# Attention and MLP on one core: the second products of a block queued straight behind its first products, in place of being mixed with the next block's first products

## The chip, the cores and the metric

The kernel runs on one core of a Trainium2 chip. The metric is device time in microseconds of one execution, the median of several runs.

## The reference

An attention over 8 batches, 12 heads, 448 positions of 64 values feeds an MLP with a squared ReLU:

```
scores = (q @ k^T) / sqrt(64);  e = exp(scores - m)
attn   = e / (sum(e) + exp(-m) + 1e-9)          # softmax with one added to the sum
x      = (attn @ v), heads put side by side     # 3584 tokens x 768
g      = max(x @ w_in, 0) ** 2                  # 3584 x 2048
out    = g @ w_out                              # 3584 x 768, float32
```

## The kernel before

**Attention.** The work is cut into units `(b, pr, q0, n)`: batch, pair of heads, first query, number of queries. Batch 0 is done in 12 half units of 192 and 256 queries, batches 1 to 7 in 6 units of 448 queries each, so `NU` is 54 and the main loop runs over `i` from 0 to 54. In turn `i` TensorE does `scores(u, et, 0)` and `scores(u, et, 1)` of the unit `i` (tile `sp`, L174 in batches 0 and 1, L186 from batch 2 on), then for the unit before it the row sums (tile `mp`, L230) and the values (tile `xp`, L222). ScalarE takes the exponential of each score tile (`et`, L154), and makes the reciprocal of the row sums with a logarithm and an exponential (`lnz` L233, `rcp` L234). VectorE adds the chunks of `et` in three steps (`es`, L199 and L201), and `normalise` (L242) multiplies `xp` by `rcp` into `xt`, which is the input of the MLP.

**MLP.** It runs over blocks of tokens: 128, 256 (both of batch 0), then 512 and 384 in turn, the last of 512. `mlp_in` makes the first products: 16 tiles of 6 matmuls each (L257), each tile cleared at zero by VectorE (`rt`, L266) and squared by it (`g`, L268). Only in the first block ScalarE does `rt`. `mlp_out` makes the second products: for each 128 tokens 16 matmuls of 512 columns and 16 of 256 (L280), each tile scaled by ScalarE into `ot` (L284), and then stored by SyncE (L296). A block's first products need `xt` of its tokens; its second products need all 16 tiles of its `g`.

**Buffers.** The row sums (`zp`), the tiles of both products and the transposes of batches 0 and 1 all take their PSUM tiles in turn from one pool, `m_psum`, of three buffers. Scores have two buffers (`s_psum`), the values one (`x_psum`), `g` two for each of its names.

**Order.** The order is written out by hand (`manual_schedule`), and every engine executes its own instructions in program order. The MLP is a filler: `mlp_in` and `mlp_out` are generators that yield after every matmul with its nominal time (columns / 2.4 in ns), and `drain(ns)` lets the queued work run until that much has been issued. A turn spends its `share` in five parts:

```
scores(u, et, 0); drain(share * 0.45); scores(u, et, 1)
row_sums(prev, pes); values(prev, pet, xp, 0); values(prev, pet, xp, 1)
drain(share * 0.15)
for step in range(3): add_chunks(...); drain(share * (0.15, 0.1, 0.15)[step])
normalise(prev, xp, rcp)
```

`ready` says after which unit which work is queued; `share` is then the work left, divided by six. In the kernel before, `ready` queues the first products of a block together with the second products of the block before it, and `queue` puts both into one generator, `mixed`. It takes the one whose done share is smaller and lets it go on to the end of its PSUM tile (the flag that the generators yield beside the time). So the second products of a block come some six turns after its first products, and after the last turn there remain a mixed piece (second products of 384 tokens, first products of 512) and the second products of 512.

**Loads.** GpSimd loads `v`, the weights and the copies `stage` of q and k; SyncE loads q and k transposed from `stage` (L129, `transposed_loads`, after the unit `pr` = 2 of the batch before), and stores the output on the same queue.

Of the kernel before, what the change touches and what calls it, by code (L numbers as in the profile page):

```python
# [15 lines left out]
def kernel(  # L16
# [12 lines left out]
    NT, DM = out.shape  # L29
    DF = moe_w_in.shape[1]  # L30
    NPAIR = H // 2
    DCH = DM // 128
    NFFB = DF // 128
# [41 lines left out]
    def load_v(b, p0, p1):  # L75
        hs = slice(2 * p0, 2 * p1)
        if b not in vns:
            vns[b] = v_pool.tile([P, H, RUN, D], FP16, name="vn")
        nc.gpsimd.dma_start(out=vns[b][:, hs], in_=v_r[b, :, hs])  # L79
# [29 lines left out]
    def stage(b):  # L109
        for n, t in (("q", q), ("k", k)):  # L110
            st = nc.dram_tensor(f"stage_{n}{b}", (TOTAL,), FP16, kind="Internal").ap()
            stages[n, b] = st
            src = t.rearrange("b h s d -> (b h s d)")
            lo = b * HSD - FRONT
            hi = min(lo + TOTAL, B * HSD)
            m = (hi - lo) // 1024 * 1024
            for x, y in ((lo, lo + m), (lo + m, hi)):
                if y > x:
                    w = min(y - x, 1024)
                    nc.gpsimd.dma_start(out=st[x - lo:y - lo].rearrange("(r w) -> r w", w=w),  # L120
                                        in_=src[x:y].rearrange("(r w) -> r w", w=w))
            if hi < lo + TOTAL:
                nc.gpsimd.dma_start(out=st[hi - lo:TOTAL].rearrange("(r w) -> r w", r=1),
                                    in_=src[0:lo + TOTAL - hi].rearrange("(r w) -> r w", r=1))
# [11 lines left out]
    def regroup(b, pr):  # L136
        for name in "qk":
            f = flat.tile([P, RUN, 2, D], FP16, name=f"flat{name}")
            nc.vector.tensor_copy(f, naturals[name, b, pr].rearrange("p h t d -> p t h d"))
            flats[name, b, pr] = f  # L140

    def transposes(b, pr):
        tp = m_psum.tile([128, 2, 512], FP16, name="mp")
        for i, name in enumerate("qk"):
            for s in range(RUN):
                nc.tensor.transpose(tp[:, i, P * s:P * s + P], flats[name, b, pr][:, s], ident[0:P, 0:P])
        if b not in qks:
            qks[b] = qk_pool.tile([128, 3, COLS], FP16, name="qk")
        nc.vector.tensor_copy(qks[b][:, 0:2, pr * S:(pr + 1) * S], tp[:, :, 0:S])
# [92 lines left out]
        nc.vector.tensor_mul(xts[b // 2][:, pr, c:c + n], xp[:, 0:n], rcp[:, 0:n])  # L242

    gts = {}

    def mlp_in(t0, n):
        gt = gts[t0] = []
        xt, x0 = xts[t0 // (2 * S)], t0 % (2 * S)  # L250
        per = max(1, 512 // n) if n < 384 else 1
        for f0 in range(0, NFFB, per):
            hp = m_psum.tile([128, 512], FP32, name="mp")
            for j in range(per):
                fb = f0 + j
                for dc in range(DCH):
                    nc.tensor.matmul(hp[:, j * n:(j + 1) * n], win[:, dc, fb * 128:(fb + 1) * 128],  # L257
                                     xt[:, dc, x0:x0 + n], start=(dc == 0), stop=(dc == DCH - 1))
                    if j < per - 1 or dc < DCH - 1:
                        yield n / 2.4, False  # L260
            m = per * n
            rt = r_pool.tile([128, 512], FP16, name="rt")
            if t0 == 0:
                nc.scalar.activation(out=rt[:, 0:m], in_=hp[:, 0:m], func=AF.Relu)  # L264
            else:
                nc.vector.tensor_scalar(out=rt[:, 0:m], in0=hp[:, 0:m], scalar1=0.0, scalar2=None, op0=ALU.max)  # L266
            g = g_pool.tile([128, 512], FP16, name=f"g{f0}")
            nc.vector.tensor_mul(g[:, 0:m], rt[:, 0:m], rt[:, 0:m])  # L268
            for j in range(per):
                gt.append(g[:, j * n:(j + 1) * n])  # L270
            yield n / 2.4, True

    def mlp_out(t0, n):
        gt = gts.pop(t0)
        for ts in range(n // 128):
            ot = osb_pool.tile([128, DM], FP32, name="ot")
            for n0, n1 in ((0, 512), (512, DM)):
                op = m_psum.tile([128, 512], FP32, name="mp")
                for fb in range(NFFB):
                    nc.tensor.matmul(op[:, 0:n1 - n0], gt[fb][:, ts * 128:(ts + 1) * 128], wout[:, fb, n0:n1],  # L280
                                     start=(fb == 0), stop=(fb == NFFB - 1))
                    if fb < NFFB - 1:
                        yield (n1 - n0) / 2.4, False
                nc.scalar.activation(out=ot[:, n0:n1], in_=op[:, 0:n1 - n0], func=AF.Copy, scale=OUT_SCALE)  # L284
                if n1 < DM:
                    yield (n1 - n0) / 2.4, True
            c = t0 + ts * 128
            end = c + 128
            while c < end:
                b = c // S  # L290
                step = RUN if b in ON_PE else 2
                rows = out[b * S:(b + 1) * S, :].rearrange("(p t) m -> t p m", t=step)
                t, p = c % S // (S // step), c % (S // step)
                m = min(S // step - p, end - c)
                o = c + 128 - end
                nc.sync.dma_start(out=rows[t, p:p + m, :], in_=ot[o:o + m, :])  # L296
                c += m
            yield (DM - 512) / 2.4, True


    warm = consts.tile([128, 512], FP16)
# [24 lines left out]

    work, left = [], [0.0]

    def mixed(parts):

        gens = [[0.0, total, gen] for gen, total in parts]
        while gens:
            g = min(gens, key=lambda g: g[0] / g[1])
            for ns, end in g[2]:
                g[0] += ns
                yield ns
                if end:
                    break
            else:
                gens.remove(g)  # L340

    def queue(parts):
        both = []
        for part, t0, n in parts:
            total = (NFFB * DCH * n if part == 1 else n // 128 * NFFB * DM) / 2.4
            both.append(((mlp_in if part == 1 else mlp_out)(t0, n), total))
            left[0] += total
        work.append(mixed(both))

    def drain(ns):  # L350
        while work and ns > 0:
# [9 lines left out]
    units += [(b, pr, 0, S) for b in range(1, B) for pr in range(NPAIR)]  # L361
    NU = len(units)

    ready = {NPAIR - 1: [(1, 0, 128)], 2 * NPAIR - 1: [(1, 128, 256), (2, 0, 128)]}
    last, t0 = (2, 128, 256), 384
    for b in range(1, B):
        n = 384 if b % 2 == 0 else 512
        ready[(b + 2) * NPAIR - 1] = [last, (1, t0, n)]
        last = (2, t0, n)
        t0 += n  # L370


    regroup_at = {pr - 2: (0, pr) for pr in range(2, NPAIR)}
    transpose_at = {pr - 1: (0, pr) for pr in range(1, NPAIR)}
# [4 lines left out]
    def keep_warm(n):  # L379
        wp = m_psum.tile([128, 512], FP32, name="mp")  # L380
        for _ in range(n):
            nc.tensor.matmul(wp, warm[:, 0:128], warm, start=True, stop=True)
# [8 lines left out]
    for i in range(NU + 1):  # L391
        u = units[i] if i < NU else None
        prev = units[i - 1] if i > 0 else None
        xp = rcp = None
        if prev:
            pet, pes = et, es
            xp = x_psum.tile([128, 512], FP32, name="xp")
        if u:
            b, pr = u[0:2]
            if pr == 0 and 0 < b and b + 1 < B:  # L400
                load_v(b + 1, 0, NPAIR)
                stage(b + 1)
            et = e_pool.tile([P, RUN * 2 * S], FP16, name="et")
            es = e_pool.tile([P, 4 * S], FP16, name="es")
            scores(u, et, 0)
            if i == 0:
                keep_warm(8)
            if i in transpose_at:
                transposes(*transpose_at[i])
            if i in regroup_at:  # L410
                regroup(*regroup_at[i])
            if i < NPAIR:
                keep_warm(1)
            drain(share * 0.45)
            scores(u, et, 1)
        if prev:
            rcp = row_sums(prev, pes)
            values(prev, pet, xp, 0)
            values(prev, pet, xp, 1)
            if i < NPAIR:  # L420
                keep_warm(1)
        drain(share * 0.15)
        for step in range(3):
            if u:
                add_chunks(u, et, es, step)
            drain(share * (0.15, 0.1, 0.15)[step])
        if prev:
            normalise(prev, xp, rcp)
            if i - 1 in ready:
                queue(ready[i - 1])  # L430
                share = left[0] / NPAIR
        if u and b and pr == 2 and b + 1 < B:
            transposed_loads(b + 1)
    queue([last])
    drain(1e12)


# [28 lines left out]
```

## Time and profile before

| | us |
|---|---|
| median of 3 runs | 442.65 |
| lowest and highest | 441.81, 442.74 |
| the profiled execution | 441.81 |
| its span, first to last instruction | 440.0 |

Outside the span of the profiled execution lie 1.81 us. Busy times of an engine are the sum of its instructions. TensorE's matmuls overlap, and their ends are modelled, so the time that a run of matmuls takes is read from one start to the next start and not from a duration.

### The profile page before, as it was taken

To read this page: it belongs to the slowest core of one execution; us is meant where nothing else is said; L and a number is where in the kernel's file an instruction comes from. 1 tells how busy PE (TensorE), PEld (TensorE's weight loads), DVE (VectorE), ACT (ScalarE), POOL (GpSimd) and SP (SyncE) were. 2 spreads that over 40 slices of the span, in tenths; PEclk is the share of its full clock that TensorE was granted. 3 is DMA by queue.
4 is the path that set the end of the run, shared out by engine and by line. 5 is a ranking of instruction groups with operands and counts; after the bars stand their busy time and mean duration, and the time that the engine had idled before them with its cause. 6 is when DMAs were issued, how large, how long until landed. Compare 5 with 4: busy or idle time off the path is not lost.

```text
span 440.0 us, 7510 instructions
## 1 busy us (share of the span) xinstructions
PE 425.2 (97%) x3147; PEld 231.1 (53%) x3147; DVE 244.2 (55%) x487; ACT 247.8 (56%) x361; POOL 33.4 (8%) x52
## 2 busy tenths in 40 slices
PE   7989899999999999999999999999999998999996
PEld 3556455554545555455455555455455554555564
DVE  3857668586656553664675655475475545345500
ACT  2889887856575556646566555755666655100011
POOL 7441100100010000100010000300000000000000
PEclk9989999999999999999999999999999999999999
DMA  9999999795078801956039901958100001011122
GB/s 169 197 197 204 209 213 188 128 203 119 1 127 184 176 13 45 203 122 141 1 67 196 214 13 36 179 124 149 38 36 14 26 36 37 36 37 36 37 72 72
DMA packets 78946, 47.22 MB, mean 107 GB/s; under 512 B 50624, under 2 KB 74944, under 8 KB 78528
## 3 DMA queue, kind: packets, MB, share of 16 engines
q0 software_dynamic: 24608, 22.40, 31.9%
q1 hardware_dynamic: 54304, 24.34, 24.1%
q8 instruction: 24, 0.39, 0.4%
q14 instruction: 10, 0.08, 0.1%
HBM read 45.71 MB, written 19.32 MB: 148 GB/s over the span
## 4 chain that ended last, share of the span: by engine, by line
PE 83%; DMA 12%; DVE 1%; POOL 1%; SPq 1%; issue 1%; ACT 0%; POOLq 0%
PE mp L280 33%; PE mp L257 31%; PE sp L186 8%; PE xp L222 6%; DMA win<-in_moe_w_in_dram 6%; DMA wout<-in_moe_w_out_dram 5%; PE mp L230 3%; DMA qk<-stage_k 1%; SPq L129 1%; PE sp L174 1%; DVE rt L266 1%; ACT et L154 0%; POOL qn L91 0%; DVE g L268 0%; POOL vn L79 0%
## 5 line engine op out<-in xcount | busy, mean ns | idle before, releaser
L154 ACT ACTIVATE et<-sp 112x896 f16<-112x896 f32 (+2 forms) x192 | 166.1, 913 | 120.8 <-PE sp L186 105.9
L257 PE MATMUL mp<-xt,win 128*128 128x512 f16 (+3 forms) x864 | 162.1, 334 | 1.7 <-DVE xt L242 1.7
L280 PE MATMUL mp<-wout,g 128*128 128x512 f16 (+1 forms) x896 | 160.3, 326 | 0.2 <-DMA wout<-in_moe_w_out_dram 0.2
L266 DVE TENSOR_SCALAR rt<-mp 128x512 f16<-128x512 f32 (+1 forms) x120 | 76.2, 635 | 128.3 <-PE mp L257 126.6
L280 PEld LDWEIGHTS <-g 128*128 128x128 f16 x896 | 83.9, 98 | 63.9 <-issue 11.3
L257 PEld LDWEIGHTS <-win 128*128 128x128 f16 x864 | 79.3, 99 | 70.5 <-issue 11.4
L199 DVE TENSOR_TENSOR es<-et 112x896 f16<-112x896 f16 x84 | 50.9, 620 | 21.9 <-ACT et L154 21.9
L284 ACT ACTIVATE ot<-mp 128x512 f32<-128x512 f32 (+1 forms) x56 | 27.2, 486 | 62.0 <-PE mp L280 62.0
L268 DVE TENSOR_TENSOR g<-rt 128x512 f16<-128x512 f16 (+1 forms) x124 | 49.5, 399 | 7.0 <-ACT rt L264 2.7
L222 PE MATMUL xp<-et,vn 112*64 112x448 f16 (+2 forms) x432 | 45.6, 332 | 1.3 <-DVE xt L242 1.3
L186 PE MATMUL sp<-qk 64*112 64x224 f16 x576 | 43.9, 268 | 0.9 <-ACT et L154 0.5
L186 PEld LDWEIGHTS <-qk 64*112 64x112 f16 x576 | 27.3, 128 | 27.6 <-issue 26.9
L233 ACT ACTIVATE lnz<-mp,one_b 128x448 f32<-128x448 f32 (+2 forms) x54 | 32.1, 595 | 2.6 <-PE mp L230 2.4
L242 DVE TENSOR_TENSOR xt<-xp,rcp 128x448 f16<-128x448 f32 (+2 forms) x54 | 30.5, 566 | 0.0
L222 PEld LDWEIGHTS <-vn 112*64 112x64 f16 x432 | 24.0, 110 | 11.9 <-DVE xt L242 1.3
L234 ACT ACTIVATE rcp<-lnz 128x448 f32<-128x448 f32 (+2 forms) x54 | 28.9, 535 | 2.0 <-DVE xt L242 0.3
L201 DVE TENSOR_TENSOR es<-es 112x896 f16<-112x896 f16 x42 | 26.1, 622 | 0.7
L79 POOL DMA_DIRECT2D vn<-in_v_dram x10 | 8.9, 888 | 232.2 <-PE xp L222 218.9
L230 PE MATMUL mp<-es,ones 112*64 112x448 f16 (+2 forms) x108 | 19.4, 356 | 2.2 <-DVE es L207 1.6
L174 PE MATMUL sp<-qk 64*112 64x192 f16 (+2 forms) x144 | 17.7, 313 | 1.6 <-ACT et L154 1.3
L174 PEld LDWEIGHTS <-qk 64*112 64x112 f16 x144 | 7.3, 126 | 10.0 <-issue 6.9
L230 PEld LDWEIGHTS <-ones 112*64 112x64 f16 x108 | 6.1, 106 | 11.3 <-issue 5.1
(32 smaller groups left out, 85.3 us busy)
## 6 DMA issues: line engine op xcount, KB each, us to landing
out_dram<-ot SPq DMA_DIRECT2D x12, 384.0 KB, 2.3
vn<-in_v_dram POOLq DMA_DIRECT2D x6, 672.0 KB, 7.2
stage_q<-in_q_dram POOLq DMA_DIRECT2D x5, 676.0 KB, 9.7
stage_k<-in_k_dram POOLq DMA_DIRECT2D x5, 676.0 KB, 12.4
win<-in_moe_w_in_dram POOLq DMA_DIRECT2D x8, 384.0 KB, 14.8
wout<-in_moe_w_out_dram POOLq DMA_DIRECT2D x4, 768.0 KB, 19.4
out_dram<-ot SPq DMA_DIRECT2D x8, 288.0 KB, 2.6
out_dram<-ot SPq DMA_DIRECT2D x8, 192.0 KB, 2.8
```

Source lines behind the costliest of these rows:

```text
L154: nc.scalar.activation(out=out_, in_=in_, func=AF.Exp, scale=scale)
L174: nc.tensor.matmul(sp[:, h, o:o + n], qk[r, 1, x + P * kk:x + P * kk + P], qk[r, 0, x + q0:x + q0 + n], start=True, stop=True)
L186: nc.tensor.matmul(sp[:, odd, h * (S // 2):(h + 1) * (S // 2)], qk[r, which, kx:kx + 2 * P - 1:2], qk[r, 0, x:x + S // 2], start=True, sto ...
L199: nc.vector.tensor_add(f[:, step], e[:, 2 * step], e[:, 2 * step + 1])
L222: nc.tensor.matmul(xp[64 * h:64 * h + 64, 0:n], vns[b][:, 2 * pr + h, kk, :], of_head(chunk(et, u, c, kk), u, h), start=(kk == 0), stop=(k ...
L230: nc.tensor.matmul(zp[64 * h:64 * h + 64, 0:n], ones, of_head(total, u, h), start=True, stop=True)
L233: nc.scalar.activation(out=lnz[:, 0:n], in_=zp[:, 0:n], func=AF.Ln, bias=one_b)
L242: nc.vector.tensor_mul(xts[b // 2][:, pr, c:c + n], xp[:, 0:n], rcp[:, 0:n])
L257: nc.tensor.matmul(hp[:, j * n:(j + 1) * n], win[:, dc, fb * 128:(fb + 1) * 128], xt[:, dc, x0:x0 + n], start=(dc == 0), stop=(dc == DCH - 1))
L266: nc.vector.tensor_scalar(out=rt[:, 0:m], in0=hp[:, 0:m], scalar1=0.0, scalar2=None, op0=ALU.max)
L268: nc.vector.tensor_mul(g[:, 0:m], rt[:, 0:m], rt[:, 0:m])
L280: nc.tensor.matmul(op[:, 0:n1 - n0], gt[fb][:, ts * 128:(ts + 1) * 128], wout[:, fb, n0:n1], start=(fb == 0), stop=(fb == NFFB - 1))
```

## The change

The generators yield times alone; `mixed` is gone; `queue` appends each part by itself, and parts run one after the other. `ready` now queues a block's second products right behind its own first products. After unit 11 three parts are queued: the first products of 256 tokens, then the second products of 128 and those of 256. Nothing is left over for the end but the last block's own two parts. Buffers, pools and all instructions are the same in number and size; the ones product takes its PSUM tile from `m_psum` and `m_psum` has three buffers in both versions.

```diff
-    def mixed(parts):
-        gens = [[0.0, total, gen] for gen, total in parts]
-        while gens:
-            g = min(gens, key=lambda g: g[0] / g[1])
-            for ns, end in g[2]:
-                g[0] += ns
-                yield ns
-                if end:
-                    break
-            else:
-                gens.remove(g)
-
-    def queue(parts):
-        both = []
-        for part, t0, n in parts:
-            total = (NFFB * DCH * n if part == 1 else n // 128 * NFFB * DM) / 2.4
-            both.append(((mlp_in if part == 1 else mlp_out)(t0, n), total))
-            left[0] += total
-        work.append(mixed(both))
+    def queue(part, t0, n):
+        work.append((mlp_in if part == 1 else mlp_out)(t0, n))
+        left[0] += (NFFB * DCH * n if part == 1 else n // 128 * NFFB * DM) / 2.4
...
-    ready = {NPAIR - 1: [(1, 0, 128)], 2 * NPAIR - 1: [(1, 128, 256), (2, 0, 128)]}
-    last, t0 = (2, 128, 256), 384
+    ready = {NPAIR - 1: [(1, 0, 128)],
+             2 * NPAIR - 1: [(1, 128, 256), (2, 0, 128), (2, 128, 256)]}
+    t0 = 384
     for b in range(1, B):
         n = 384 if b % 2 == 0 else 512
-        ready[(b + 2) * NPAIR - 1] = [last, (1, t0, n)]
-        last = (2, t0, n)
+        ready[(b + 2) * NPAIR - 1] = [(1, t0, n), (2, t0, n)]
         t0 += n
...
             if i - 1 in ready:
-                queue(ready[i - 1])
+                for part in ready[i - 1]:
+                    queue(*part)
                 share = left[0] / NPAIR
...
-    queue([last])
     drain(1e12)
```

More of the change, by code (lines that the diff above doesn't have):

```diff
@@ L259, in mlp_in @@
                     if j < per - 1 or dc < DCH - 1:
-                        yield n / 2.4, False
+                        yield n / 2.4
             m = per * n
@@ L270, in mlp_in @@
                 gt.append(g[:, j * n:(j + 1) * n])
-            yield n / 2.4, True
+            yield n / 2.4
     def mlp_out(t0, n):
@@ L282, in mlp_out @@
                     if fb < NFFB - 1:
-                        yield (n1 - n0) / 2.4, False
+                        yield (n1 - n0) / 2.4
                 nc.scalar.activation(out=ot[:, n0:n1], in_=op[:, 0:n1 - n0], func=AF.Copy, scale=OUT_SCALE)
                 if n1 < DM:
-                    yield (n1 - n0) / 2.4, True
+                    yield (n1 - n0) / 2.4
             c = t0 + ts * 128
@@ L297, in mlp_out @@
                 c += m
-            yield (DM - 512) / 2.4, True
+            yield (DM - 512) / 2.4
     warm = consts.tile([128, 512], FP16)
```

## Prediction

> **What bounds the kernel now.** I read the page first, then TensorE's waits, then TensorE's timeline start by start.
>
> ```profile
> PE 425.2 (97%) x3147; PEld 231.1 (53%) x3147; DVE 244.2 (55%) x487; ACT 247.8 (56%) x361; POOL 33.4 (8%) x52
> L266 DVE TENSOR_SCALAR rt<-mp 128x512 f16<-128x512 f32 (+1 forms) x120 | 76.2, 635 | 128.3 <-PE mp L257 126.6
> ```
>
> TensorE is busy 97%, VectorE and ScalarE 55%; VectorE's `rt` waits for matmuls, not the reverse. A busy 97% can hide slow matmuls, so I take starts from the timeline, here of the end of the kernel:
>
> ```profile
> 400.75 2.75 PE L257 MATMUL mp<-xt,win 128*128 128x512 f16 x12
> 403.34 3.62 PE L280 MATMUL mp<-wout,g 128*128 128x512 f16 x16
> 406.79 5.34 PE L257 MATMUL mp<-xt,win 128*128 128x512 f16 x24
> 411.97 1.91 PE L280 MATMUL mp<-wout,g 128*128 128x256 f16 x16
> 413.72 1.46 PE L257 MATMUL mp<-xt,win 128*128 128x512 f16 x6
> ```
>
> Twelve matmuls of 512 columns take 403.34 - 400.75 = 2.59 us, 0.216 each; sixteen of L280 3.45, 0.216 again; 256 columns take 1.75 / 16 = 0.109; 384 columns 0.163 (18 from 333.38 to the scores at 336.40, less 0.09 that the step into the scores always adds). The switch between L257 and L280 costs nothing. The same spacings hold inside the attention turns. So TensorE streams at one rate, mixed or not, and the total of its work is fixed: what the change can move are the places where the stream stands. After turn 13, where the two orders part, I find these, as start-to-start excess over the usual step (four score matmuls or a group of eight: 0.52; row sums to values: 0.21):
>
> ```profile
> 60.05 1.38 PE L257 MATMUL mp<-xt,win 128*128 128x256 f16 x11
> 61.35 0.79 PE L174 MATMUL sp<-qk 64*112 64x448 f16 x4
> 62.07 0.38 PE L230 MATMUL mp<-es,ones 112*64 112x448 f16 x2
> ...
> 76.07 0.30 PE L186 MATMUL sp<-qk 64*112 64x224 f16 x1
> 76.80 0.59 PE L186 MATMUL sp<-qk 64*112 64x224 f16 x7 [0.42 <-DMA qk<-stage_k]
> 77.32 1.38 PE L257 MATMUL mp<-xt,win 128*128 128x256 f16 x11
> ...
> 369.99 2.11 PE L257 MATMUL mp<-xt,win 128*128 128x384 f16 x12
> 372.71 0.38 PE L230 MATMUL mp<-es,ones 112*64 112x448 f16 x2 [0.60 <-DVE es L201]
> 374.11 0.95 PE L222 MATMUL xp<-et,vn 112*64 112x448 f16 x8 [1.01 <-DVE xt L242]
> ```
>
> - At 61.35 the second scores of a turn take 0.72 in place of 0.52: the exponentials of the first scores are not out of the two `sp` buffers yet, because only 1.30 us of MLP (11 matmuls) stood between. So at 66.70, 72.54 and 78.62: 4 x 0.2 = 0.8 us.
> - 55.14: a wait for `wout`, 0.33. 67.42: values behind the VectorE queue, 0.47. 76.07: the transposed `qk` of batch 2 lands late, 1.25 - 0.52 = 0.73. 80.41: scores with no MLP before them, 0.25. Sum 1.78.
> - 226.27 and 327.25, at the end of two blocks' shares: scores directly behind values, 0.44 each, 0.88.
> - 369.99 and 372.71, the last turn: row sums wait for an `es` that stands behind an `rt`, `g` pair on VectorE (2.72 less 12 x 0.163 and 0.09 is 0.67), then values wait for `normalise`, which stands behind the next pair (1.40 - 0.21 = 1.19): 1.86.
>
> Together 5.3 us, 1.2% of the span.
>
> **The change, part by part.** The counts of matmuls per turn follow from the shares and from the order in which the changed program's instructions stand.
>
> *Turns 13 to 18.* They now also hold the second products of 256 tokens: 32 x 0.216 + 32 x 0.109 = 10.4 us, taken out of the later turns and, step by step, out of the stretch after the last turn. No time is won by the move itself. But a turn there holds 25.6 / 6 = 4.27 us nominal in place of 2.56: 18 matmuls (2.0 us) stand between the two scores in place of 11 (1.3), which covers the 0.2. By adding up the turns from 47.23 I get the turn that needs the transposed `qk` at 83.1 in place of 76.07; the loads wait for the `stage` copies issued at 48.75 and 49.27, before the orders part, so they still land at 76.8: 6 us of cover. On SyncE's queue they stand behind no output of their own block, since second products now come three turns later. The first L280 falls at about 64 us, against the last `wout` at 55.7: 8 us of cover. If that cover were gone, the 0.33 would return. Gain 0.8 + 1.78 = 2.58.
>
> *Ends of shares.* Second products end a block now; 8 to 15 matmuls of 256 columns (0.9 to 1.7 us) are left over between values and the next scores, which covers 0.44 twice. The price: at three block ends where nothing stood before the scores, the 0.09 of stepping into them is paid anew, 0.3 in all. The new block then starts with first products, the sixth matmul of which needs the newest `normalise`. From 224.68 I read its time: scores at T, `normalise` from T + 3.41 to T + 4.03 (228.09, 0.62 long). The sixth matmul comes at T + 0.53 + 0.21 + 0.86 (values) + 0.96 (eight left over) + 0.52 (scores) + 5 x 0.216 = T + 4.16. It just fits. Gain 0.88 - 0.3.
>
> *The last turn.* Only second products are there now, so no `rt` stands before `es` and `normalise` on VectorE: by T + 4.03 both are done, and row sums come at T + 4.9. Gain 1.86.
>
> *First products in one piece.* This is what the change costs. In the first three turns of a block all filler is first products: 34 matmuls, 5.67 tiles a turn. VectorE spends 0.59 + 0.28 = 0.87 us a tile at 384 columns (335.96 to 336.54 to 336.82) and 0.72 + 0.34 = 1.06 at 512 (311.45 to 312.17 to 312.51), and 2.3 us for three adds and `normalise` (343.40 to 345.13, and 0.55). A 384 turn loads VectorE with 5.67 x 0.87 + 2.3 = 7.2 us and TensorE with 34 x 0.163 + 2.3 = 7.9; a 512 turn 8.3 against 9.6. So TensorE stays the bound, at 91% and 86%. But a tile may start only when the tile three before it in `m_psum`, row sums counted, has been read. I walked three turns with these spacings, `rt` starting 0.20 after the last matmul's stream (375.97 to 376.17). At 512 nothing waits. At 384 one tile in the second turn finds its buffer about 0.1 late and the row sums behind it again 0.1: 0.2 a block, three blocks, 0.6 us. No row of the trace has such a run of first products under attention, so both ends stay open: 0 (VectorE catches up beside scores and values), and 0.67 per turn, the row sums' wait at 372.71, in all 18 such turns, 12.1. I take the walk's 0.6, as VectorE's total fits.
>
> *Second products in one piece* put `ot` of 0.59 and 0.38 us, one pair a turn more, on ScalarE, whose turn holds 4 x 0.87 + 0.67 + 0.68 = 4.8 us; 5.8 fits turns of 7 to 9. Covered. Output stores land in about 2.5 us, each 128 tokens every turn or so; two `ot` buffers cover them. GpSimd's queue keeps its order. *The stretch after the last turn* is shorter by what went earlier and streams as before: a tile 1.30 of TensorE, 1.06 of VectorE.
>
> Sum: 5.3 - 0.3 - 0.6 = 4.4 us less. On the profiled execution, 441.81 - 4.4 = 437.4 (span 435.6); on the median of the runs, 0.84 above it, 438.2. I say 437.8.
>
> A rule speaks against the change. The Trainium skill, Perfetto Trace Analysis, section Optimization Strategy, says that where the most-contended engine changes between regimes, interleaving the regimes can help. Undoing an interleaving should then make VectorE the bound in one half of a block and cost time. This case's before shows no such regimes, since mixed stretches run with TensorE at the stream's rate; whether the separated ones become regimes is just what the walk decides.
>
> **Rivals.**
> - *VectorE sets the pace in the first products.* The adds stand between `rt`s, the ring of three runs out every turn, and `m_psum` is what TensorE waits for. For it: 91% load and a margin of 0.1 us in the walk. Against: VectorE's sum fits. At 0.67 a turn it costs 12.1, and with the 5.0 gained 448.9. It decides from 5.0 / 18 = 0.28 us a turn on: slower. Chance 0.11.
> - *Only the later waits go.* The early turns stay bound by ScalarE (17.6 of 21.3 us busy from 55.7 to 77) or by the loads, and give nothing: 1.86 + 0.88 - 0.3 - 0.6 = 1.8 gained, 440.0. Against: six us of cover. Chance 0.14.
> - *Nothing happens.* The work is the same and the stream is full; new waits of the size of the old replace them: 441.8 to 442.6. Chance 0.04.
> - My forecast, 0.71, by itself 436.6 to 439.2.
>
> **How the numbers follow.** A change of 0.2%, 0.9 us, is about what this measurement can tell from none. Forecast and second rival are faster, 0.85; same 0.04; slower 0.11. The range reaches from all 5.3 gained and none lost, on the profiled execution (436.5), to the second rival and a turn's losses above it, 441.0; above that lies 0.15.
>
> **What would show it.** Right: the waits list of TensorE without L230 on `es` L201, `xp` on `xt` and `qk` on DMA after turn 13; spacings of 0.216 and 0.163 inside first products; the last turn's row sums at once. Wrong: a repeating wait of L256 (as L257 is then numbered) or L230 on `rt`, or VectorE's busy share over 95% in the first three turns of a block.

## The result, and the profile after

| | before | after |
|---|---|---|
| median, us | 442.69 (441.81 to 443.46, 4 runs) | 436.62 (436.03 to 437.17, 4 runs) |
| profiled execution, us | 441.81 | 437.17 |
| its span | 440.0 | 435.4 |

The ratio is 0.9863, with a 95% interval of 0.9839 to 0.9888: 1.4% faster. The forecast was 437.8, with a span of 435.6; the median lies 1.2 us under it, close to the lower end of the stated range (436.5).

The first page lines of after:

```profile
PE 423.7 (97%) x3147; PEld 230.4 (53%) x3147; DVE 244.4 (56%) x487; ACT 248.2 (57%) x361; POOL 33.2 (8%) x52
L265 DVE TENSOR_SCALAR rt<-mp 128x512 f16<-128x512 f32 (+1 forms) x120 | 76.0, 633 | 37.3 <-PE mp L256 34.6
```

The busy shares say nothing of the change: 97% before and after. What has moved in them is VectorE's idle time ahead of `rt`: 37.3 us where it had 128.3, since `rt`s now come in bursts and then not at all. All that TensorE still waits for, by its view of waits:

```profile
PE mp L256 <- DVE xt L242: 1.7, 2, 1.5
PE mp L230 <- DVE es L207: 1.6, 3, 0.9
PE mp L146 <- DVE flatk L139: 1.4, 3, 0.6
PE sp L174 <- ACT et L154: 1.3, 4, 0.4
PE mp L363 <- DVE warm L301: 1.2, 1, 1.2
PE sp L174 <- DVE qk L149: 0.2, 1, 0.2
```

Row sums on `es` L201, values on `xt`, scores on the load of the transposed `qk` and second products on `wout` are gone; the rest lies before the two orders part. The three places that the prediction showed, in TensorE's timeline of after (the first or last line of a view counts only what starts inside the window asked for, so `x6` can be part of a group of eight):

```profile
61.89 0.59 PE L174 MATMUL sp<-qk 64*112 64x448 f16 x4
62.41 1.70 PE L256 MATMUL mp<-xt,win 128*128 128x256 f16 x14
63.95 0.59 PE L279 MATMUL mp<-wout,g 128*128 128x512 f16 x2
...
82.91 0.59 PE L186 MATMUL sp<-qk 64*112 64x224 f16 x8
83.43 2.23 PE L279 MATMUL mp<-wout,g 128*128 128x512 f16 x13
85.59 0.59 PE L186 MATMUL sp<-qk 64*112 64x224 f16 x8
...
381.96 3.43 PE L279 MATMUL mp<-wout,g 128*128 128x256 f16 x21
385.32 0.38 PE L230 MATMUL mp<-es,ones 112*64 112x448 f16 x2
385.53 0.73 PE L222 MATMUL xp<-et,vn 112*64 112x448 f16 x6
```

Each group of scores gives way to the next after 0.52 us. The first second product starts at 63.95, and the turn that needs the transposed `qk` at 82.91. The last turn's row sums follow the fillers at once, and the values follow them after 0.21.

From turn 13, where the orders part, to the last matmul, the kernel before took 435.70 - 47.23 = 388.47 us and this one 431.07 - 46.93 = 384.14: 4.33 less. The other 0.30 of the spans' 4.6 was there at turn 13 already, where both kernels had issued the same work, and has nothing to do with the change.

### The profile page after: what moved, and what is told of

It reads as the page before. It is cut to its first block, busy times and chain, and to the rows that moved or that the text cites. A ratio compares the mean times of both kernels' runs of the same rounds, so it can differ in the third digit from the quotient of the medians.

```text
span 435.4 us, 7530 instructions
## 1 busy us (share of the span) xinstructions
PE 423.7 (97%) x3147; PEld 230.4 (53%) x3147; DVE 244.4 (56%) x487; ACT 248.2 (57%) x361; POOL 33.2 (8%) x52
## 4 chain that ended last, share of the span: by engine, by line
PE 91%; ACT 3%; DMA 2%; issue 1%; DVE 1%; POOL 1%; ACTq 0%; POOLq 0%
PE mp L279 34%; PE mp L256 34%; PE sp L186 9%; PE xp L222 8%; PE mp L230 3%; DMA kn<-in_k_dram 2%; PE sp L174 2%; ACT et L154 2%; ACT lnz L233 1%; PE mp L146 1%; DVE es L203 0%; ACT rcp L234 0%; POOL qn L91 0%; DVE xt L242 0%; POOL vn L79 0%
## 5 line engine op out<-in xcount | busy, mean ns | idle before, releaser
L256 PE MATMUL mp<-xt,win 128*128 128x512 f16 (+3 forms) x864 | 156.4, 334 | 1.7 <-DVE xt L242 1.7
L279 PE MATMUL mp<-wout,g 128*128 128x512 f16 (+1 forms) x896 | 154.2, 326 | 0.0
L279 PEld LDWEIGHTS <-g 128*128 128x128 f16 x896 | 84.2, 98 | 63.2 <-issue 9.6
L256 PEld LDWEIGHTS <-win 128*128 128x128 f16 x864 | 78.2, 99 | 71.9 <-issue 12.7
L265 DVE TENSOR_SCALAR rt<-mp 128x512 f16<-128x512 f32 (+1 forms) x120 | 76.0, 633 | 37.3 <-PE mp L256 34.6
L186 PE MATMUL sp<-qk 64*112 64x224 f16 x576 | 42.8, 268 | 0.0
L201 DVE TENSOR_TENSOR es<-es 112x896 f16<-112x896 f16 x42 | 26.2, 623 | 1.0
```

The source lines that it names most:

```text
L186: nc.tensor.matmul(sp[:, odd, h * (S // 2):(h + 1) * (S // 2)], qk[r, which, kx:kx + 2 * P - 1:2], qk[r, 0, x:x + S // 2], start=True, sto ...
```

## The experiments

**The two kernels again.** No edit.

> The kernel before itself, unchanged, to see by how much its span moves from one execution to the next. The traces show a gain of 4.6 us of span (440.0 to 435.4), the medians 6.1. My theory: the kernel before has waits on transfers (wout 0.33 us, the transposed qk 0.73 us) whose size changes with the landing, so its span at one granted clock spreads by over 0.5 us and its median span lies up to 1.5 us above the 440.0 of its profiled execution. Rival: the medians differ by the granted clock alone (0.995 or 1.0), and spans of one clock agree within 0.3 us.

> The changed kernel, unchanged, beside the kernel before on one chip. Theory: 436.0 to 437.2 us in two groups by the granted clock (434.3 and 435.3 us of span so far), nothing between, because no wait on a transfer is left after turn 13. Rival: spans spread as those of the kernel before do.

Medians were 443.15 and 437.68 us; against the kernel before on the same chip (442.97), the changed kernel has a ratio of 0.9881 (0.9855 to 0.9907). The spans, sorted by each execution's mean granted clock:

| mean clock | spans before, us | spans after, us |
|---|---|---|
| 1.000 | 440.1 to 442.0 (9) | 434.2 to 434.6 (3) |
| 0.996 | 439.9 to 442.1 (12) | 435.2 to 435.9 (4) |
| 0.992 | 440.1 to 441.3 (5) | 437.0 |
| 0.988 | 441.1, 441.4 | 437.9 |

(Before: 71 executions on four chips, of which the table has those at the same clocks as after's; after: 9 of its 10, the tenth, 435.4, at 0.995.) The first expectation held: before spreads by 1 us and more at one clock, and its median span in this run, 441.4, is 1.4 above the 440.0 of the profiled execution. The second held in part: after's span follows the clock, but in more steps than the two groups forecast, and it spreads by 0.7 us at 0.996. Before does not get shorter at a full clock; why is taken up below, under the term that was mis-sized. So the distance is 5.7 us at 0.996 (median of each group) and 6.8 at full clock, and the profiled execution of before was one of the shortest.

**Mixing off, the lag kept.** The diff is against the changed kernel.

```diff
-             2 * NPAIR - 1: [(1, 128, 256), (2, 0, 128), (2, 128, 256)]}
-    t0 = 384
+             2 * NPAIR - 1: [(1, 128, 256), (2, 0, 128)]}
+    last, t0 = (2, 128, 256), 384
...
-        ready[(b + 2) * NPAIR - 1] = [(1, t0, n), (2, t0, n)]
+        ready[(b + 2) * NPAIR - 1] = [last, (1, t0, n)]
+        last = (2, t0, n)
...
+    queue(*last)
     drain(1e12)
```

> Mixing taken off alone: the kernel before's lag stays (a block's second products are queued with the next block's first products, second products first), but the two run one after the other. Theory (what wins is when second products come, not that they are unmixed): the early stalls of 2.0 to 2.6 us stay, the last turn again holds first products and its row sums and values wait about 1 to 2 us, only the 0.88 at the ends of shares goes, and 0.6 to 1 us of waits for the ring come in runs of first products: 439.5 to 440.5 us of span, 0 to 1 us under the kernel before. Rival (mixing itself costs): within 1 us of the changed kernel, 435.4 to 436.4.

443.19 us, ratio 1.0007 (0.9985 to 1.0029): no gain, where the expectation left room for up to 1 us. Its last turn:

```profile
368.44 3.75 PE L256 MATMUL mp<-xt,win 128*128 128x384 f16 x22
373.06 0.38 PE L230 MATMUL mp<-es,ones 112*64 112x448 f16 x2 [0.87 <-DVE es L201]
374.46 0.95 PE L222 MATMUL xp<-et,vn 112*64 112x448 f16 x8 [1.02 <-DVE xt L242]
```

These are the waits of the kernel before, here without any mixing. So not mixing, with the lag kept, wins nothing on balance; what wins is when second products come.

**The early part undone.** The second products of the 256 block go back behind turn 18.

```diff
-             2 * NPAIR - 1: [(1, 128, 256), (2, 0, 128), (2, 128, 256)]}
+             2 * NPAIR - 1: [(1, 128, 256), (2, 0, 128)]}
...
-        ready[(b + 2) * NPAIR - 1] = [(1, t0, n), (2, t0, n)]
+        ready[(b + 2) * NPAIR - 1] = ([(2, 128, 256)] if b == 1 else []) + [(1, t0, n), (2, t0, n)]
```

> The changed kernel with only its early part undone: the second products of the 256 block are held back from turns 13 to 18 to turn 19. Nothing is mixed. Theory (the moved work covers the score buffers and the landing of qk): the stalls of 0.2 us in four turns, 0.73 on qk and 0.25 at scores without MLP before them come back, 1.8 to 2.2 us more span than the changed kernel at one clock (437.2 to 437.6). Rival (the gain comes from not mixing): no more than 0.3 us more.

441.55 us, 3.9 over the changed kernel's 437.68 beside it: more than forecast. In its trace the early stalls are back and sum to 2.3 us (four of 0.1 to 0.2 at second scores, 0.35 at values, 0.70 at `qk`, 0.31 at scores without MLP before them, 0.20 at the scores after `qk`). Another 0.9 us stands at a place that the expectation missed:

```profile
145.01 0.59 PE L186 MATMUL sp<-qk 64*112 64x224 f16 x8
145.53 0.38 PE L230 MATMUL mp<-es,ones 112*64 112x448 f16 x2
145.74 0.92 PE L222 MATMUL xp<-et,vn 112*64 112x448 f16 x8
146.60 0.28 PE L279 MATMUL mp<-wout,g 128*128 128x256 f16 x1
146.81 0.82 PE L186 MATMUL sp<-qk 64*112 64x224 f16 x8
147.56 0.99 PE L256 MATMUL mp<-xt,win 128*128 128x384 f16 x5
```

and on VectorE:

```profile
147.87 0.62 DVE L201 TENSOR_TENSOR es<-es 112x896 f16<-112x896 f16 x1
148.41 0.61 DVE L242 TENSOR_TENSOR xt<-xp,rcp 128x448 f16<-128x448 f32 x1
```

The longer share of that block left one matmul over at its end in place of eight or more. Five matmuls of the new block go, and the sixth needs the `normalise` that ends at 148.41 + 0.61, 4.0 us after the scores at 145.01: 0.71 of waiting, and 0.23 at the scores before. That wait is the prediction's sum for the end of a share, with its cover taken away. The other 0.7 of the 3.9 is not told apart. The distance also goes with the clock: at 0.992 it is some 2.4 us (439.4, 439.5 and once 442.6 against 437.0), at 0.996 over 4 (440.1 and 441.0 against 435.2 to 435.9).

**The last turn alone.** The kernel before, mixed but for the last six turns, which do first products and then second products.

```diff
     def queue(parts):
+        if len(parts) == 2 and parts[1] == (1, 2688, 384):
+            for part in parts[::-1]:
+                queue([part])
+            return
         both = []
```

> The kernel before, mixed as it was, with the work of the last six turns alone put one after the other: first products of the 384 block, then the second products of the 512 block before it. Theory: the last turn holds second products only, and the 1.86 us that its row sums and values waited for VectorE go; 0.2 to 0.4 us of ring waits come in: 1.4 to 1.9 us less span than the kernel before at one clock (about 438.3). Rival (the last turn waits for its exponentials anyway): no change within 0.4 us.

441.57 against 443.28 us, ratio 0.9968 (0.9953 to 0.9983): 1.4 us less by the ratio, 1.7 by the medians. In its trace the last turn has no wait (row sums at 373.27, values at 373.49), so the 1.86 is real; 0.70 of it comes back at 328.98, where the block's first products again start with nothing left over before them. The rival is out. The same trace also shows the wait for `wout`, in an execution whose clock was full from 20 to 40 us. First the same place in the kernel before, whose clock was 0.91 there, then this run:

```profile
54.48 1.04 PE L280 MATMUL mp<-wout,g 128*128 128x512 f16 x4
55.69 0.59 PE L280 MATMUL mp<-wout,g 128*128 128x512 f16 x2 [0.17 <-DMA wout<-in_moe_w_out_dram]
```

```profile
53.08 1.04 PE L280 MATMUL mp<-wout,g 128*128 128x512 f16 x4
56.12 0.59 PE L280 MATMUL mp<-wout,g 128*128 128x512 f16 x2 [2.00 <-DMA wout<-in_moe_w_out_dram]
```

**One `rt` of each 384 block on ScalarE.**

```diff
-            if t0 == 0:
+            if t0 == 0 or (n == 384 and f0 == 4):
                 nc.scalar.activation(out=rt[:, 0:m], in_=hp[:, 0:m], func=AF.Relu)
```

> The changed kernel with the clearing at zero (rt) of one first-product tile of each 384 block, the third (f0 = 4), on ScalarE in place of VectorE. In the trace the sixth tile's rt comes 0.15 us late in each 384 block and the row sums behind it 0.09. Theory (VectorE's backlog at a ring of three): with one rt of 0.56 us less in its queue both waits go, 3 x 0.24 = 0.7 us less span than the changed kernel at the same clock (434.7 where it has 435.4). Rival: ScalarE's exponentials are pushed back by the rt and the scores wait in its place, no change or up to 1 us more.

(`f0` counts tiles from zero, so this is the fifth tile of the block and not the third, as the expectation has it.) 436.74 us against 437.68 for the changed kernel and 442.97 for the kernel before: ratio 0.9846 (0.982 to 0.9871). Its trace has no stall of over 0.04 us after the two at the start of turn 13 (0.62 and 0.37), which the changed kernel has too. At full clock its spans are 433.8 and 434.1, against 434.2 to 434.6. It has the lowest median here, but its runs spread by 1.96 us, more than the 0.94 between the medians; that both waits went is read from the trace.

**More work on VectorE.** Each tile of `g` is computed twice, in both orders.

```diff
             nc.vector.tensor_mul(g[:, 0:m], rt[:, 0:m], rt[:, 0:m])
+            nc.vector.tensor_mul(g[:, 0:m], rt[:, 0:m], rt[:, 0:m])
```

> The kernel before with every tile of g computed twice on VectorE (same values, 0.28 to 0.34 us more per first-product tile). VectorE's load of a block of six turns goes from about 28 to 33 of 50 us, so mixed with second products it stays hidden: 0 to 1.5 us more than the kernel before.

> The changed kernel with every tile of g computed twice. A turn of first products loads VectorE with 8.8 us against TensorE's 7.9 at 384 columns and 10.2 against 9.6 at 512. Theory (VectorE's load per turn decides, and the margin was some 10%): it becomes the bound in the first three turns of each block and in the last block's first products: 6 to 12 us more than the changed kernel, 443 to 449 us, so about as slow as the kernel before or slower. Rival (the ring and the second products behind absorb it): under 2 us more.

446.99 us mixed and 453.05 separate (two executions): 3.9 more than before (443.12 beside it), and 15.4 more than after (437.68 on another chip). Both were dearer than expected, and the order turned round: mixed is now 6 us faster. The waits of the separate kernel begin with

```profile
PE mp L256 <- DVE rt L265: 5.2, 12, 0.7
PE mp L230 <- DVE rt L265: 4.6, 10, 0.6
```

and its windows, the first one over the first products of a 384 block, show VectorE at 22.54 of 26 us:

```profile
146.00:172.00 26.00, 24.07 (x186) 13.84 (x184) 22.54 (x52) 15.37 (x22) 1.96 (x3) 1.00 0.98 175
```

The mixed kernel stands behind VectorE at 68.8, 101.6 and 110.2 us, in the last turn and just after it, and nowhere between. So the prediction's first rival names a true mechanism, which had no room in the changed kernel: with 0.28 to 0.34 us a tile more, it decides.

**Two tiles for the products.** The row sums get a bank of their own, the products' ring goes from three to two.

```diff
-    m_psum = ctx.enter_context(tc.tile_pool(name="m_psum", bufs=3, space=bass.MemoryType.PSUM))
+    m_psum = ctx.enter_context(tc.tile_pool(name="m_psum", bufs=2, space=bass.MemoryType.PSUM))
+    z_psum = ctx.enter_context(tc.tile_pool(name="z_psum", bufs=1, space=bass.MemoryType.PSUM))
...
-        zp = m_psum.tile([128, 512], FP32, name="mp")
+        zp = z_psum.tile([128, 512], FP32, name="zp")
```

> The kernel before with two tiles for the products in place of three, and a bank of its own for the row sums. Mixing puts a second-product tile of 1.75 or 3.45 us between many first-product tiles, so rt is mostly in time; runs of up to four first-product tiles remain: 0 to 6 us more than the kernel before, 442 to 448 us.

> The changed kernel with two tiles for the products and a bank of its own for the row sums. Theory (the third tile is what lets VectorE fall behind by its adds): a tile may now start only when rt of the tile but one before is done, a slack of 0.17 us at 384 columns and 0.35 at 512 against a backlog of up to 1.5 and 0.9 us in the walk: about 1.1 us in each of nine 384 turns and 0.5 in each of nine 512 turns, 8 to 15 us more than the changed kernel, 445 to 452 us, and the order of mixed and separate turns round. Rival (the order of second products wins whatever the ring): still 3 us or more under the mixed kernel with the same ring.

453.43 us mixed, 449.24 separate (two executions each): 10.2 more than the kernel before (443.28) and 11.6 more than after. The separate one lost what the walk forecast. The mixed one lost far more than expected, and so stays the slower by 4.2: the rival held. Its waits, first line, against the separate one's:

```profile
PE mp L258 <- ACT ot L285: 4.3, 8, 0.6
```

```profile
PE mp L257 <- DVE rt L266: 4.8, 13, 0.6
```

With two tiles a first product that follows a second product stands behind `ot`, which on ScalarE's queue stands among the exponentials; I had counted `rt` alone. That line is 4.3 of the 10.2 us; the rest is spread over smaller waits. Mixing is no guard for a short ring.

**The copies of the next batch ahead of its `v`.** The kernel before, two lines swapped.

```diff
-                load_v(b + 1, 0, NPAIR)
                 stage(b + 1)
+                load_v(b + 1, 0, NPAIR)
```

> The kernel before with one swap in the turns that load the next batch: the copies stage of q and k are issued ahead of the load of v, which on GpSimd's queue waits for the values of the batch before (from 36.5 to 47.8 us in turn 12). So the copies for batch 2 can start some 11 us earlier and the transposed qk should land well before turn 18. Open is why the medians moved by 6 us where the forecast's waits sum to 4.4: in traces of the unchanged early order without a low granted clock from 20 to 40 us the wait for wout is 1.4 to 2.2 us and not 0.33, and spans of the kernel before do not shrink where the clock is full. Theory (landings set the pace of turns 13 to 18 there, qk the last of them): the 0.73 us on qk go and up to 2 us more with them, 0.7 to 2.5 us less than the kernel before, and spans now fall with a fuller clock. Rival (the copies only push wout back, or the pace is set elsewhere): within 0.5 us, or slower.

466.7 us, the middle of four executions at a mean clock of 0.966 to 0.973 (two more, at 0.958 and 0.959, took 472.19 and 474.02); ratio 1.0531 (1.0494 to 1.0567): the wrong way.

```profile
PE sp L186 <- DMA qk<-stage_k: 22.5, 2, 20.1
PE mp L280 <- DMA wout<-in_moe_w_out_dram: 1.3, 1, 1.3
```

The copies are issued at 38.1 and 39.8 us in place of 48.8 and 49.3, and yet the transposed `qk` lands 20 us later: SyncE's first transposed load runs from 61.4 for 28.5 us where it took 3.6. Why it is that slow beside `v` and the weights isn't shown. What it does show is that TensorE stands at that turn for as long as `qk` is late; it doesn't show that an earlier landing would win anything.

## Why the prediction was right

- *The early turns.* The stalls went, and the cover is as reckoned: the turn that needs `qk` at 82.91 (forecast 83.1), the first L279 at 63.95 (forecast about 64), the transposed loads starting at 64.80 and 68.52 (64.21 and 67.85 before). Putting the early part back cost 3.9 us, more than the 2.58 forecast for it; 0.9 of that is the experiment's own.
- *Ends of shares.* No wait at 88.80, where first products follow nine left over matmuls, nor at the like places later; with one left over, 0.9 us is paid.
- *The last turn.* Row sums and values wait for nothing; moving that alone won 1.4 us, net of 0.70 that it brought; by the prediction's terms 1.86 - 0.70 = 1.16 was due, which lies inside the interval.
- *First products in one piece.* The walk forecast that at 384 columns one tile in the second turn is about 0.1 late and the row sums behind it again 0.1, and at 512 nothing waits. In after, second turn of the 384 block:

```profile
149.72 1.95 PE L256 MATMUL mp<-xt,win 128*128 128x384 f16 x11
151.60 0.59 PE L186 MATMUL sp<-qk 64*112 64x224 f16 x8
152.13 2.76 PE L256 MATMUL mp<-xt,win 128*128 128x384 f16 x15
154.82 0.59 PE L186 MATMUL sp<-qk 64*112 64x224 f16 x8
155.43 0.38 PE L230 MATMUL mp<-es,ones 112*64 112x448 f16 x2
155.62 0.73 PE L222 MATMUL xp<-et,vn 112*64 112x448 f16 x5
```

```profile
153.43 0.62 DVE L242 TENSOR_TENSOR xt<-xp,rcp 128x448 f16<-128x448 f32 x1
153.97 0.55 DVE L265 TENSOR_SCALAR rt<-mp 128x384 f16<-128x384 f32 x1
154.55 0.36 DVE L267 TENSOR_TENSOR g<-rt 128x384 f16<-128x384 f16 x1
154.82 0.55 DVE L265 TENSOR_SCALAR rt<-mp 128x384 f16<-128x384 f32 x1
```

Fifteen matmuls take 154.82 - 152.13 = 2.69, where 15 x 0.163 + 0.09 is 2.54: 0.15 late, because the last tile's buffer is free only when the `rt` behind `normalise` ends, at 153.97 + 0.55. Then row sums come 0.61 after the scores and not 0.52: 0.09. At 253.00 and 353.88 the same again, and nowhere else: 3 x 0.24 = 0.72 against the forecast 0.6. VectorE's load was also as reckoned: busy 7.15 of 8.09 us from 148.41 to 156.50, where the prediction had 7.2 of 7.9.
- *The sum.* 4.33 us from turn 13 on, against 4.4. That it fits to 0.07 is in part luck of the pair: both profiled executions had a low clock from 25 to 35 us, as had the one that the waits were read from. By the medians the kernels are 6.1 us apart, more than the 5.3 that the prediction took for all that could be won.
- *The rivals.* VectorE as the bound needs 0.28 us a turn, and of the eighteen turns in after fifteen cost nothing and three 0.24. That only the later waits go is out by the turns from 57 to 88 us, which stand nowhere; that nothing happens, by the interval.

**The term that was mis-sized** is the one of the transfers. The prediction took 0.33 us for `wout` from an execution in which the granted clock was 0.91 from 20 to 40 us, so that TensorE came late to the wait. In the trace of the kernel before run again, with a low clock from 25 to 35 and from 45 to 55 us, there is no such wait at all. In three traces with the same early order and a full clock there (the last turn alone, two tiles mixed, more VectorE work mixed) the excess at that place is 2.17, 1.4 and 2.0. That would account for spans of before that don't fall with a fuller clock, and for medians 6.1 us apart where the two profiled executions are 4.6 apart: time lost to a low clock ahead of the wait is taken off the wait. `wout` can't be all of it. The kernel with the early part undone has no wait for `wout`, as its second products begin at 69.82 us, and its spans don't fall either: 439.3 to 439.5 at 0.991 and 0.992, with one of 442.6, and 439.5 to 440.5 at 0.998. It does wait for the transposed `qk`, 0.70 us in a trace with two low stretches; how long at a full clock no trace of it shows. That these landings set the pace is read from spans and traces; the experiment that was to test it by itself failed in another way, so it is argued and not shown.

**The rule weighed.** The Trainium skill, Perfetto Trace Analysis, section Optimization Strategy, says that interleaving may help where the most-contended engine changes between regimes. It did here where the other engine's load in a separated stretch was reckoned above TensorE's (8.8 against 7.9 us a turn): with `g` made twice, undoing the interleaving cost 6 us. In the kernel as it is VectorE is busy 17.39 of 22.20 us in the first products of a 384 block (144.27 to 166.47 of after), and the interleaving hid no more than 0.7 us. The same section's rule that a bubble which repeats can mean too few buffers fits the 0.15 us at the same tile of three blocks, which stand where the ring of three runs out; no run here has a ring of four.

## What to carry to other kernels

Where the bound engine streams at one rate in every stretch, a reordering is worth the sum of the places where it stands, read as start-to-start excess over the usual step; find each place's cover in the new order and walk one turn of the tightest engine before believing the rest. Fillers are worth most where nothing else covers a chain: between two groups of scores, ahead of a block's first use of a fresh result, and in the last turn. A wait for a transfer is sized from several executions, since one with a low clock can hide it.

## What the runs showed that was not expected

- The changed kernel's span went from 434.2 to 434.6 us at a mean clock of 1.000 to 437.9 at 0.988, and the kernel before's, over the same clocks, stayed at 440 to 442.
- Waits of 0.2 us are not seen as idle time: a group of four score matmuls that stood that long shows as 0.79 us busy in place of 0.58.
- One transposed load took 28.5 us on SyncE's queue in place of 3.6, when the copies were issued 10 us earlier.
